# Another phase for the planner's instruction fetches, and shorter 2-KB loads

## The chip, the cores and the metric

One core of a Trainium2 chip runs the whole kernel. The metric is the device time of one execution in microseconds (us), as the median of the runs of a kernel.

## The reference

What is computed is an attention in which a query sees only the keys of its own cluster, and two feed-forward layers behind it. Cut to what matters:

```python
def _attn_ref(q, k, v, centroids):            # q, k, v: 2 x 8 x 768 x 64; centroids: 8 x 16 x 64
    q_assign = np.argmax(np.einsum('bhsd,hcd->bhsc', q_n, c_n), axis=-1)   # q_n, k_n, c_n: rows
    k_assign = np.argmax(np.einsum('bhsd,hcd->bhsc', k_n, c_n), axis=-1)   # of length one
    mask = q_assign[:, :, :, None] == k_assign[:, :, None, :]
    scores = np.where(mask, scale * np.matmul(q, k.transpose(0, 1, 3, 2)), -1e9)
    attn = np.exp(scores - np.max(scores, axis=-1, keepdims=True))
    attn = attn / (np.sum(attn, axis=-1, keepdims=True) + 1e-09)
    return np.matmul(attn, v)
def _moe_ref(x, w_in, w_out):                 # x: 1536 x 512; w_in: 512 x 2048; w_out: 2048 x 512
    h = x @ w_in
    return (h * (1.0 / (1.0 + np.exp(-h)))) @ w_out
def _moe2_ref(x, w_in, w_out, alpha):         # the same shapes
    h = x @ w_in
    return (np.maximum(h, 0.0) + alpha * np.minimum(h, 0.0)) @ w_out
```

The weights come as 64-bit floats, 8 MB for each of the four matrices.

## The kernel before

**Attention.** The work is cut into 96 units, one for a tile of 128 query rows and a head. TensorE makes the scores of a unit from four matmuls (L793 and L797, in `front`): one pair adds the one-hot cluster codes and so the mask, one pair the products. VectorE scales them and takes the minimum (L807), ScalarE takes the exponential (L812) and the high half of the split in two half-precision parts (L819), and VectorE the low half (L821). SyncE then issues a DMA transpose of both parts (L827, in `front_t`), and 18 matmuls with the values (L839, in `back`) read what it wrote. Two units later than the scores, as the code is written, but in the order that a planner sets. Before the units the keys, queries and values are scaled and split and the cluster codes made: K and Q are transposed once for the products (L638, L730) and once with their codes (L684, L746). L498 is a small matmul that sums a scale's squares over the partitions, and its input comes from ScalarE (L611, L648, L713 or L945).

**Weights.** Each of the four weight matrices is loaded in eight pieces of 1 MB (L893). A piece of 64-bit floats is turned into 32-bit ones by ScalarE (L904, L908) and VectorE (L915, L918), scaled by a sum of squares (TensorE's L953 with VectorE's L955 for the first two matrices, ScalarE's L945 for the others), and split in two half-precision parts (L930 on ScalarE, L931 on VectorE).

**Layers.** The first feed-forward layer takes chunks of one or two tiles as soon as their attention is done (matmuls L1187 and L1218, in `layer1`), and the second takes three blocks of 512 rows at the end (L1289 and L1320, in `layer2`). Its results leave by 12 stores (L1328).

**Order.** No engine's order is the one that the code is written in. When all instructions have been recorded, `plan_order` (L313) makes a `Plan`. `data_deps` finds who needs whom, `run` places all instructions by a list schedule with the costs of `costs`, and `improve` repeats this 60 times, forward and backward with a little noise, and keeps the order whose planned end is the earliest. Each engine then runs that order, with SyncE, which issues all DMAs, among them. In `costs` a load has an issue time of 0.47 us, a latency, and a time in the queue by its size and a rate (L104 to L107). In `run` the planner counts TensorE's records, two for each matmul (the weight load and the matmul). When the count passes 256 it takes an instruction fetch to begin. A load or transpose that is then in flight is made later by 1.1 or 0.4 us, and so are those who wait for it and the queue behind it.

Of the kernel before, what the change touches and what calls it, by code (L numbers as in the profile page):

```python
# [48 lines left out]
class Plan:  # L49
# [27 lines left out]
    def costs(self, i):  # L77
        aps = [a for a in list(i.ins) + list(i.outs) if hasattr(a, "bass_ap")]
        n = max(self.size(a) for a in aps) if aps else 1
        kind, e = type(i).__name__, self.engine(i)  # L80
        wide = all(a.dtype in (F16, BF16) for a in aps)
        ptr = sum(hasattr(a, "bass_ap") for a in list(i.ins)[1:]) if n > 1 else 0
        if kind == "InstTensorScalarPtr":
            ptr = sum(self.size(a) == 1 for a in i.ins if hasattr(a, "bass_ap")) if n > 1 else 0
        many = len(list(i.outs)) > 1
        if e == "PE":
            mv = [a for a in i.ins if hasattr(a, "bass_ap")][0]
            return (max(0.025, 0.001 + self.size(mv) * (8 if mv.dtype == F32 else 1) / 2330.0),)
        if e == "DVE":
            if kind == "InstTensorCopy":  # L90
                return (0.15 + n / (3840.0 if wide else 1920.0),)
            if kind == "InstMemset":
                return (0.06 + n / 1000.0,)
            return (0.145 + n / 955.0 + (0.06 * ptr if kind == "InstTensorScalarPtr" else 0) + 0.06 * many,)
        if e == "Activation":
            return (0.19 + n / 1205.0 + 0.09 * min(1, ptr) + (0.06 if many else 0),)
        if e == "Pool":
            if kind == "InstTensorTensor":
                return (0.19 + n / 530.0,)
            return ((0.1 if kind == "InstMemset" else 0.19) + n / 1215.0 + 0.08 * min(1, ptr),)  # L100
        n = max(self.size(a) for a in aps)
        if kind == "InstDmaTransposeAnt":
            return (1.3 if n < 1400 else 1.42, 1.3, n / 750.0)
        rows = [a for a in i.ins][0]  # L104
        run = list(rows.ap)[-1][1] * 4
        rate = 400.0 if run >= 4096 else 290.0 if run >= 2048 else 380.0
        return (0.47, 1.3, n * 512 / 1000.0 / rate)  # L107

    @staticmethod
# [93 lines left out]
    def run(self, prio):  # L203
# [17 lines left out]
        port = [0.0] * ne  # L221
        other = {1: 3, 3: 1}
        window = [0, False, 0.0]
        fetched, flight = 190, []
        for n in range(N):
            if not left[n]:
                heapq.heappush(later[self.eng[n]], (0.0, prio[n], n))
        for _ in range(N):
# [36 lines left out]
            if kind == "PE":  # L265
# [12 lines left out]
                if fetched >= 256:  # L278
                    fetched -= 256
                    flight = [x for x in flight if x[0] > s]  # L280
# [1138 lines left out]
```

## Time and profile before

| | us |
|---|---|
| median of 3 runs (783.64 to 786.57) | 785.26 |
| the profiled execution | 784.7 |
| its span, from the first instruction to the last | 782.8 |
| TensorE (PE) busy | 679.5 |
| VectorE (DVE) busy | 541.3 |
| ScalarE (ACT) busy | 466.5 |
| GpSimd (POOL) busy | 136.2 |

The profile gives busy time by engine, who waited for whom, and for each DMA the time from its issue to its landing. PEld is TensorE's weight load, and SPq the queue of SyncE. An instruction is named by its line in the kernel's file. The granted clock of TensorE is a share of 2.4 GHz: 1.00, or 0.50, which is 1.2 GHz; in between are means over a stretch. The tile "arena" is the one large buffer in which nearly everything lies, so a DMA "arena<-arena" is a transpose. Queue q8 carries the fetches of instructions.

### The profile page before, as it was taken

What the parts mean: (1) busy time and instruction counts of PE and PEld (TensorE: products, weight loads), DVE (VectorE), ACT (ScalarE), POOL (GpSimd) and SP (SyncE); (2) the same over time, 40 slices, a digit from 0 to 9 for tenths busy, and PEclk for the clock granted to TensorE, in tenths of its full rate; (3) what the DMA queues carried; (4) which work ended last, traced back from release to release, by engine and by line L of the source; (5) the groups of instructions that cost most, each with busy time, mean ns of one, the idle gap of its engine ahead of it and who ended that gap; (6) DMA issues with size and microseconds to landing.
All of it is one profiled execution on the core that took longest, in us unless ns stands there. A gap on an engine that the chain in (4) does not pass through costs nothing.

```text
span 782.8 us, 16346 instructions
## 1 busy us (share of the span) xinstructions
PE 679.5 (87%) x6730; PEld 475.0 (61%) x6730; DVE 541.3 (69%) x992; ACT 466.5 (60%) x757; POOL 136.2 (17%) x237
## 2 busy tenths in 40 slices
PE   0254559679999999998999999888999999999998
PEld 0243448568887878887788898774444444444443
DVE  4689998898779578867876886878970385018700
ACT  6875976777778667756765898997640141012200
POOL 3562131123404732121130001000000000000000
PEclk9999978899999999999999999999999999999999
DMA  7989997989999996996898986452000000000000
GB/s 216 300 201 294 300 214 125 156 168 152 165 160 158 186 162 129 155 167 125 138 142 135 243 225 187 160 172 100 1 15 27 14 1 0 28 28 1 0 28 27
DMA packets 241593, 101.85 MB, mean 130 GB/s; under 512 B 217328, under 2 KB 227568, under 8 KB 241392
## 3 DMA queue, kind: packets, MB, share of 16 engines
q1 hardware_dynamic: 241520, 100.83, 60.4%
q8 instruction: 52, 0.85, 0.4%
q14 instruction: 21, 0.17, 0.1%
HBM read 44.08 MB, written 3.15 MB: 60 GB/s over the span
## 4 chain that ended last, share of the span: by engine, by line
PE 36%; ACT 7%; DMA 5%; DVE 2%; issue 1%; POOL 0%; SPq 0%; ACTq 0%
PE w L1320 11%; PE w L1289 10%; PE m L1320 5%; PE m L1289 5%; DMA arena<-in_moe_w_out_dram 2%; PE w L1218 2%; ACT arena L904 2%; ACT arena L908 2%; ACT arena L945 1%; PE w L1187 1%; DMA arena<-arena 1%; DMA arena<-in_moe_w_in_dram 1%; PE x L839 1%; PE s L793 1%; PE s L797 1%
## 5 line engine op out<-in xcount | busy, mean ns | idle before, releaser
L1218 PE MATMUL w<-arena 128*128 128x256 f16 (+1 forms) x1248 | 150.1, 258 | 3.7 <-ACT arena L1225 1.9
L1187 PE MATMUL w<-arena 128*128 128x256 f16 (+1 forms) x1200 | 142.0, 257 | 3.1 <-DVE arena L1195 1.7
L1218 PEld LDWEIGHTS <-arena 128*128 128x128 f16 x1344 | 113.2, 99 | 22.3 <-issue 5.7
L1187 PEld LDWEIGHTS <-arena 128*128 128x128 f16 x1344 | 111.9, 98 | 23.3 <-issue 8.3
L821 DVE TENSOR_TENSOR arena<-arena 128x768 f16<-128x768 f32 x96 | 96.8, 1009 | 30.4 <-ACT arena L819 30.0
L839 PE MATMUL x<-arena 128*128 128x64 f16 x1728 | 108.6, 198 | 10.1 <-DMA arena<-arena 8.0
L812 ACT ACTIVATE arena<-s,stat 128x768 f32<-128x768 f32 x96 | 85.9, 895 | 38.1 <-DVE s L807 18.4
L807 DVE TENSOR_SCALAR_CACHE_REDUCE s<-s,stat 128x768 f32<-128x768 f32 x96 | 97.6, 1019 | 12.2 <-PE s L797 10.4
L839 PEld LDWEIGHTS <-arena 128*128 128x128 f16 x1728 | 90.6, 102 | 21.2 <-DMA arena<-arena 10.9
L819 ACT ACTIVATE arena<-arena 128x768 f16<-128x768 f32 x96 | 80.3, 837 | 30.2 <-DMA arena<-arena 29.5
L1320 PEld LDWEIGHTS <-arena 128*128 128x128 f16 x576 | 56.4, 98 | 68.0
L1289 PEld LDWEIGHTS <-arena 128*128 128x128 f16 x576 | 55.7, 98 | 68.5 <-issue 2.4
L1289 PE MATMUL w<-arena 128*128 128x512 f16 x384 | 94.1, 379 | 0.0
L1320 PE MATMUL w<-arena 128*128 128x512 f16 x384 | 85.8, 379 | 0.0
L1298 DVE TENSOR_SCALAR arena<-w,stat 128x512 f32<-128x512 f32 x32 | 23.9, 747 | 78.8 <-PE w L1289 78.7
L793 PE MATMUL s<-arena 80*128 80x384 f16 x192 | 68.6, 357 | 9.9 <-ACT arena L812 9.7
L1302 ACT ACTIVATE arena<-arena,stat 128x512 f16<-128x512 f32 x48 | 34.4, 718 | 69.2 <-DVE arena L1299 69.2
L797 PE MATMUL s<-arena 128*128 128x384 f16 x192 | 68.5, 357 | 0.0
L450 POOL TENSOR_SCALAR stat<-stat 128x1 int32<-128x1 int32 x49 | 12.4, 256 | 290.1 <-DVE stat L445 197.1
L915 DVE SCALAR_TENSOR_TENSOR arena<-arena 128x1024 int32<-128x1024 int32 x32 | 41.3, 1290 | 22.2 <-ACT arena L908 22.1
L1289 PE MATMUL m<-arena 128*128 128x512 f16 x192 | 51.3, 379 | 0.1
L931 DVE SCALAR_TENSOR_TENSOR arena<-arena,stat 128x1024 f16<-128x1024 f32 x32 | 41.6, 1306 | 5.0 <-ACT arena L930 5.0
(145 smaller groups left out, 969.2 us busy)
## 6 DMA issues: line engine op xcount, KB each, us to landing
arena<-in_moe_w_in_dram SPq DMA_DIRECT2D x16, 1024.0 KB, 6.3
arena<-in_moe_w_out_dram SPq DMA_DIRECT2D x16, 1024.0 KB, 5.9
arena<-in_k_dram SPq DMA_DIRECT2D x8, 384.0 KB, 5.1
arena<-in_q_dram SPq DMA_DIRECT2D x6, 512.0 KB, 5.2
arena<-in_v_dram SPq DMA_DIRECT2D x8, 384.0 KB, 6.2
out_dram<-arena SPq DMA_DIRECT2D x12, 256.0 KB, 2.0
arena<-arena SPq DMA_TRANSPOSE x149, 4.0
arena<-in_moe_alpha_dram SPq DMA_DIRECT2D x1, 1024.0 KB, 5.3
```

Of the source, the lines that this page charges most:

```text
L793: nc.tensor.matmul(out=sc[:, j, :hs], lhsT=qt2[0:D + C, h], rhs=kt2[0:D + C, h % 2, j * hs:(j + 1) * hs], start=True, stop=False,)
L797: nc.tensor.matmul(out=sc[:, j, :hs], lhsT=qt1[:, h], rhs=kt1[:, h % 2, j * hs:(j + 1) * hs], start=False, stop=True,)
L807: nc.vector.tensor_scalar(sc[:, :, :hs], sc[:, :, :hs], nd_cols[:, H * (n % 2) + h:H * (n % 2) + h + 1], None, op0=ALU.mult, op1=ALU.min, ...
L812: nc.scalar.activation(out=view(o, F32, 2, hs), in_=sc[:, :, :hs], func=ACTF.Exp, scale=-1.0, bias=bias, accum_out=sums[n % 2][:, h:h + 1],)
L819: nc.scalar.activation(out=hl[:, 0], in_=p, func=ACTF.Copy)
L821: en.tensor_tensor(out=hl[:, 1], in0=p, in1=hl[:, 0], op=ALU.subtract)
L839: nc.tensor.matmul(out=x_ps[0][:, h], lhsT=pt[:, ph * T + t], rhs=vt[:, h % 2, t, vh], start=(i == 0), stop=(i == 3 * T - 1),)
L931: nc.vector.scalar_tensor_tensor(out=lo, in0=t, scalar=s, in1=hi, op0=ALU.mult, op1=ALU.subtract)
L1187: nc.tensor.matmul(out=hp[:, ff], lhsT=wi[:, a, kd, ff * 128:ff * 128 + 128], rhs=mov(bb, kd), start=(i == 0), stop=(i == 3 * KD - 1),)
L1218: nc.tensor.matmul(out=acc, lhsT=wo[:, a, f % 2, dt * 128:(dt + 1) * 128], rhs=g[:, f, bb], start=(i == 0), stop=(i == 3 * KF - 1),)
L1289: nc.tensor.matmul(out=hp, lhsT=in_piece(o_a + 24 * KB, f // 2)[:, a, kd, f % 2 * 128:][:, :128], rhs=x[bb][:, kd], start=(i == 0), stop=( ...
L1320: nc.tensor.matmul(out=acc, lhsT=g[:, f, a, t * 128:(t + 1) * 128], rhs=out_piece(o_w, f // 2)[:, bb, f % 2], start=(i == 0), stop=(i == 3 ...
```

## The change

Two lines of the planner. The start of its count of records goes from 190 to 50, so that it sees its first fetch at record 206 instead of 66, and all others as much later. The rates by which a load's time in the queue is worked out go from 290 to 350 (GB/s) for rows of 2 KB and from 400 to 395 for rows of 4 KB and more. No instruction is added or taken away, and the planner's order comes out new on every engine.

```diff
@@ costs
-        rate = 400.0 if run >= 4096 else 290.0 if run >= 2048 else 380.0
+        rate = 395.0 if run >= 4096 else 350.0 if run >= 2048 else 380.0
@@ run
-        fetched, flight = 190, []
+        fetched, flight = 50, []
```

Rows of 2 KB are those of the loads of the two input weights (16 loads) and of the 12 stores; the output weights and the broadcast of alpha have longer ones.

Three places of the new order follow. The first is on TensorE, where the matmuls of unit 18 with the values (tile x) begin; w0, w1 are banks of the first layer's results and s0 is a bank of scores. Before, from record 2050:

```order
L1218 MATMUL w0_68<-arena_70 128x128
L1218 LDWEIGHTS arena_70
L1218 MATMUL w1_69<-arena_70 128x128
L839 LDWEIGHTS arena_70
L839 MATMUL x_66<-arena_70 128x64
```

And now, from record 2082:

```order
L793 MATMUL s0_64<-arena_70 128x384
L797 LDWEIGHTS arena_70
L797 MATMUL s0_64<-arena_70 128x384
L839 LDWEIGHTS arena_70
L839 MATMUL x_66<-arena_70 128x64
```

The group has moved from record 2053 to 2085. In the rows where it stood there are now matmuls of L1218.

The second is SyncE's queue near the start, behind the loads of the first keys and queries; L638 and L684 are transposes of the keys, L746 that of the first queries' codes:

```order
-L638 DMA_TRANSPOSE arena<-arena 128x12x128
+L638 DMA_TRANSPOSE arena<-arena 128x12x128 x2
 L893 DMA arena<-in_moe_w_in_dram 128x4x512
-L638 DMA_TRANSPOSE arena<-arena 128x12x128
 L590 DMA arena<-in_v_dram 128x2x384
 L684 DMA_TRANSPOSE arena<-arena 128x12x128
+L893 DMA arena<-in_moe_w_in_dram 128x4x512
 L746 DMA_TRANSPOSE arena<-arena 128x8x128
-L893 DMA arena<-in_moe_w_in_dram 128x4x512 x3
+L893 DMA arena<-in_moe_w_in_dram 128x4x512 x2
```

One of the three weight loads that followed L746 now stands ahead of it, and a transpose of keys stands ahead of the weight load that it followed.

The third is ScalarE up to the first unit's exponential (L812). Before, from the fourth L648 on:

```order
L648 ACTIVATE arena,stat<-arena 128x768
L642 ACTIVATE arena<-arena 128x12x64
L654 ACTIVATE arena<-arena 128x12x64 x2
L1097 ACT_TABLE_LOAD
L1097 ACTIVATE stat<-stat 128x1
L605 ACTIVATE arena<-arena,stat 128x768
L904 ACTIVATE arena<-arena 128x1024
L908 ACTIVATE arena<-arena 128x1024
L812 ACTIVATE arena,stat<-s_65,stat 128x768
```

Now the load of the exponential's table stands behind the third L648:

```order
L611 ACTIVATE arena,stat<-arena 128x768
L648 ACTIVATE arena,stat<-arena 128x768 x3
L1097 ACT_TABLE_LOAD
L1097 ACTIVATE stat<-stat 128x1
L930 ACTIVATE arena<-arena,stat 128x1024
```

And from the fourth L648 on there stand now:

```order
L648 ACTIVATE arena,stat<-arena 128x768
L605 ACTIVATE arena<-arena,stat 128x768
L654 ACTIVATE arena<-arena 128x12x64 x2
L605 ACTIVATE arena<-arena,stat 128x768
L904 ACTIVATE arena<-arena 128x1024
L908 ACTIVATE arena<-arena 128x1024
L654 ACTIVATE arena<-arena 128x12x64
L812 ACTIVATE arena,stat<-s_65,stat 128x768
```

The table load has left the stretch ahead of the exponential, and L642 with it; a scaling (L605) and a copy of values (L654) stand there in their place.

## Rows read from the trace of the kernel before

**Rows 1.** Busy us and instructions by stretch; columns in the first row.

```profile
core 0: us, PE busy (x) PEld busy (x) DVE busy (x) ACT busy (x) POOL busy (x), PEclk, DMA share, GB/s
50.00:130.00 80.00, 50.40 (x598) 38.58 (x598) 75.39 (x157) 58.85 (x83) 24.45 (x36) 0.91 0.98 233
130.00:180.00 50.00, 38.00 (x609) 31.21 (x607) 45.66 (x83) 38.06 (x68) 13.75 (x19) 0.90 0.81 153
180.00:430.00 250.00, 239.97 (x3305) 205.23 (x3302) 191.73 (x388) 174.31 (x318) 66.94 (x99) 0.99 0.91 152
430.00:540.00 110.00, 100.35 (x979) 83.10 (x978) 88.39 (x117) 96.47 (x141) 6.55 (x22) 1.00 0.67 194
540.00:783.00 243.00, 238.95 (x1116) 108.22 (x1113) 109.96 (x165) 60.12 (x92) 1.02 (x6) 1.00 0.04 14
```

**Rows 2.** Waits of PE, 130 to 430: us in total, times, longest.

```profile
PE x L839 <- DMA arena<-arena: 8.0, 8, 2.2
...
PE w L1187 <- DMA arena<-arena: 1.4, 1, 1.4
```

**Rows 3.** Fetches (all; 149.4 to 149.6; 269.0 to 269.1), then busy sums up to two.

```profile
q8 instruction: 52, 0.85, 0.4%
...
q8 instruction: 1, 0.02, 45.8%
...
q8 instruction: 1, 0.02, 55.0%
...
0.00:149.60 149.60, 76.67 (x987) 59.09 (x987) 122.20 (x280) 111.57 (x170) 53.48 (x99) 0.95 0.94 230
0.00:269.10 269.10, 185.72 (x2672) 153.63 (x2673) 218.47 (x465) 204.15 (x338) 93.35 (x155) 0.96 0.96 202
```

**Rows 4.** Two transposes: timeline of SPq, their landing us, PE's timeline behind them.

```profile
143.15 1.42 SPq L827 DMA_TRANSPOSE arena<-arena  x1
...
146.36 1.48 SPq L827 DMA_TRANSPOSE arena<-arena  x1
...
arena<-arena SPq DMA_TRANSPOSE x1, 3.7
...
arena<-arena SPq DMA_TRANSPOSE x1, 5.6
...
152.02 1.14 PE L839 MATMUL x<-arena 128*128 128x64 f16 x18 [2.17 <-DMA arena<-arena]
```

**Rows 5.** Three loads of L893, issued one behind the other, and their landing us.

```profile
L893 SPq DMA_DIRECT2D arena<-in_moe_w_in_dram x3: 446/447/577, 34.1 to 35.3; - x3
...
DMA to landing us min/median/max: 5.9/8.5/11.0
```

**Rows 6.** Start: transpose L746 and its landing, then timelines of PE and ACT.

```profile
L746 SPq DMA_TRANSPOSE arena<-arena x1: 1862/1862/1862, 32.2 to 32.2; - x1
...
DMA to landing us min/median/max: 3.7/3.7/3.7
...
36.99 0.16 PE L498 MATMUL s<-stat,arena 128*128 128x1 bf16 x1 [8.96 <-ACT arena L648]
...
39.16 1.28 ACT L1097 ACT_TABLE_LOAD   x1
...
45.56 0.88 ACT L812 ACTIVATE arena<-s,stat 128x768 f32<-128x768 f32 x1
```

**Rows 7.** Stretches of half the granted clock; columns as in rows 1.

```profile
108.00:122.00 14.00, 9.55 (x92) 6.92 (x92) 14.00 (x25) 9.30 (x15) 2.73 (x3) 0.51 0.67 130
149.20:156.10 6.90, 4.69 (x45) 3.75 (x46) 5.85 (x9) 6.01 (x8) 0.00 (x0) 0.51 1.00 137
166.30:169.70 3.40, 3.40 (x35) 2.73 (x36) 3.16 (x7) 2.00 (x4) 0.00 (x0) 0.50 0.98 189
```

**Rows 8.** Waits of PE, 430 to 540.

```profile
PE s L498 <- ACT arena L945: 4.8, 6, 2.1
```

## The prediction

> **What bounds the kernel now.** I read the sums by stretch first, then TensorE's waits, then the transposes and the instruction fetches, then the start and the end. From 540 us TensorE is busy 238.95 of 243 us and from 180 to 430 it is busy 239.97 of 250 [rows 1]. So the total is TensorE's work plus its idle time, and a new order can only change the idle time and the clock at which the work runs. Idle are 29.6 us in 50 to 130, where VectorE is the bound (75.39 of 80), 12.0 in 130 to 180, 10.0 in 180 to 430 and 9.7 in 430 to 540 [rows 1]. In 130 to 430 the largest named cause is the units' own transposes: TensorE waited 8.0 us ahead of L839 and 1.4 ahead of L1187 for a DMA from the arena to the arena [rows 2]; two smaller kinds I leave out.
>
> Why those transposes come late is to be seen in two of them. One that was issued at 143.2 landed after 3.7 us. The one issued at 146.4 landed after 5.6, and TensorE stood 2.17 us before the matmul at 152.02 that reads it [rows 4]. Between the two ends of the second an instruction fetch of 16 KB ran, in the slice 149.4 to 149.6 [rows 3]. The profile has 52 such fetches [rows 3], one for 256 of TensorE's 13462 records (a weight load and a matmul each), and at the fetch just named TensorE had begun 987 + 987 records, which is 182 beyond a multiple of 256. By 269.1 us, beside another fetch, it had begun 2672 + 2673, which is 225 beyond one [rows 3].
>
> **The change, part by part.** *The count's start.* The planner books a fetch when its count passes 256. With 190 this is at record 66 of each 256, with 50 at record 206. The trace has it at 182 and 225 [rows 3], so the planner of before put every fetch about half a period from its true place, and the changed one puts it right to within some 25 records. What a fetch costs in the planner (0.4 or 1.1 us on a load or transpose in flight) is not changed.
>
> What this moves can be counted in the two orders. I took the first of the 18 matmuls of each unit (L839), which waits for the unit's transpose, and asked how many stand within 80 records behind record 200 of a block of 256, over the 37 blocks from 768 on. It is 28 before and 19 after. Behind record 66, where the old planner saw its fetches, it is 24 before and 35 after. So the move is as meant: units no longer begin just behind a real fetch. The wait at 152.02 is unit 18, whose group stood at record 2053 and now stands at 2085, behind the score matmuls of a later unit.
>
> Price: 8.0 + 1.4 = 9.4 us of waits [rows 2]. If they fall as the count does, by 9 in 28, this is -3.0 us. The bounds are 0 (the wait reappears at the next unit) and -9.4 (the planner now knows the landing and keeps all of them clear). I take -3.0, since the count is the only thing known of the new order at the fetches themselves.
>
> The Trainium skill speaks against this part. Runtime: NRT & Kernel Launch, section Instruction fetch mechanics, says of a refill that "The cost of crossing a 16 KiB boundary is one DMA tail-bump, mostly hidden." By that the term would be 0 and the sum 3.0 us higher. The row on the transpose that took 5.6 us beside 3.7 says otherwise: hidden from TensorE's own instruction stream, perhaps, not from a transpose in flight.
>
> *The clock behind those waits.* Granted clock was half, 1.2 GHz, in 149.2 to 156.1 and in 166.3 to 169.7, with 4.69 and 3.40 us of TensorE work in them [rows 7]. The idle stretch ahead of the first has the fetch waits in it. At 2.4 GHz the same work takes half as long, so at most (4.69 + 3.40) / 2 = 4.0 us are lost there. With the same share of 9 in 28 this is -1.3 us. Bounds: -4.0, and upward one more such stretch; the longest seen, 108 to 122, had 9.55 us of work in it [rows 7], so +4.8.
>
> *The rate of 2-KB rows.* The 16 loads of the two input weights have rows of 2 KB and 1.05 MB each. They were planned at 1.0486 MB / 290 GB/s = 3.6 us and are now planned at 3.0. Of three that queued behind each other the first landed at 34.1 + 5.9 = 40.0 us and the last at 35.3 + 11.0 = 46.3, which is 3.1 a load [rows 5]. So a load was planned 0.5 too long and is now planned 0.1 too short. No engine waits for that by itself; it only moves loads in the order, and that is the next step, so the rate is costed at nothing. The output weights' loads (2.62 to 2.65 us planned) and the stores behind the last matmuls move no other work.
>
> *The start, where both parts act.* In SyncE's queue a weight load now stands ahead of L746, the transpose of the first queries' one-hot, which so far landed 32.2 + 3.7 = 35.9 us [rows 6]. One load more ahead of it is +3.1 us, by the spacing above. TensorE began the first unit only at 36.99 though, since a matmul of L498 ahead of it waited 8.96 us for ScalarE's L648 [rows 6], and this pair stands in the same order after. So 1.1 us of the 3.1 is covered. The other 2.0 meets ScalarE, which reached the first exponential (L812) at 45.56, with the 1.28 us load of its table at 39.16 among what stood between [rows 6]. The table load now stands ahead of that stretch, where ScalarE waited anyhow. If the exponential is held by ScalarE, it comes up to 1.3 us earlier, and if by the transpose, up to 2.0 later. Behind it VectorE is full to 130 us, so either would be passed on. I take 0, since TensorE began the first unit 8.6 us ahead of the exponential; bounds -1.3 and +2.0. If the cover by L648 is gone the price is the whole 3.1.
>
> *The end of the conversions, 430 to 540.* The order of loads there is nearly the same. The waits for L945 were 4.8 us in six, the longest 2.1 [rows 8]. One such wait more or less is the bound: 0, between -2.1 and +2.1.
>
> Sum: -3.0 - 1.3 + 0 + 0 + 0 = -4.3 us. The profiled execution took 784.7 us, of which 782.8 is the span, so 780.4; it lies 0.6 us below the median of 785.3, which gives 781.0. I predict 780.7, between the two.
>
> **The rivals.** *The waits only move (about 785).* What speaks for it: 19 groups of units still stand behind a fetch, and a unit kept clear of one may meet the next. ScalarE also waits for late transposes before it can write the buffer that they read, and that does not depend on where TensorE's group stands. Against it: the count falls where the planner is right and rises where it was wrong. With the count's gain gone and the rest at 0, the time is 784.7 to 785.3. If the skill's rule on fetches held it would be this case too.
>
> *A cold stretch more (about 790).* Place: 100 to 180 us, where TensorE is busy about three quarters of the time and the clock fell three times [rows 1, 7]. The units there have moved by one or two places. Price: a stretch like 108 to 122 costs 4.8 us; where no fetch wait falls away, 785.3 + 4.8 = 790.1. It decides when the new order leaves TensorE idle before such a stretch to the degree that it is in 50 to 130, 50.40 of 80 busy [rows 1]. Against it: the planner models the clock in both versions, and the first matmul of the feed-forward layer stands at record 1194 in place of 1196, so TensorE gets no later a supply.
>
> *A larger gain (about 774).* With the landings right, the planner clears most of the waits: -8 of the 9.4, and with them most of the cold time, -3, so 785.3 - 11 = 774.
>
> **How the numbers follow.** The forecast's case, a saving of some 2.5 to 7 us, has 0.40; the larger gain 0.14; no gain 0.27; a cold stretch more, or a start that comes later, 0.19. A measurement of this kernel can tell about 0.5% from no change, 3.9 us, so faster is below 781.4. All of the larger gain and most of the forecast's case lie there: 0.48. No gain, with the small end of the forecast's case, is 0.33, and slower 0.19. The lower end of the range is 773, at the larger gain with the table load's 1.3 us; the upper end is 790, at the cold stretch. Less than one in ten lies beyond either.
>
> **What would show it.** In the new trace TensorE's waits for the arena's own transposes in 130 to 430 should be about 6.4 us instead of 9.4, with fewer matmuls of L839 found waiting two to three us behind a fetch. The fetches must still come at 170 to 230 records beyond a multiple of 256. The half clock in 140 to 170 should be shorter than 10 us. The first L812 should stand at 44 to 48 us. I am wrong if the waits for DMA fall and the time does not, for then another engine ends the wait last; or if the time falls by more than 5 us with those waits as they were, for then it is the start or the clock alone.

## The result, and the profile after

The changed kernel takes 776.5 us (median of 6 runs, 774.5 to 780.3) beside 784.8 us of the kernel before (783.5 to 787.7). The ratio is 0.989, with a 95% interval of 0.986 to 0.992, so it is faster by 8.3 us. That lies in the range, on the side that was forecast, and 4.2 us below the predicted 780.7.

The profiled execution took 777.4 us, 775.6 of them its span. Its busy times by stretch answer to [rows 1], in the same columns:

```profile
50.00:130.00 80.00, 52.39 (x618) 41.07 (x619) 73.70 (x161) 57.55 (x81) 22.30 (x38) 0.66 0.97 232
130.00:180.00 50.00, 38.60 (x559) 31.13 (x557) 41.95 (x81) 37.23 (x68) 11.90 (x16) 0.83 0.94 161
180.00:430.00 250.00, 240.18 (x3346) 206.81 (x3343) 191.21 (x389) 173.02 (x317) 72.16 (x99) 1.00 0.90 150
430.00:540.00 110.00, 107.17 (x1012) 86.36 (x1011) 92.73 (x125) 100.25 (x150) 9.61 (x22) 1.00 0.68 197
540.00:776.00 236.00, 231.42 (x1079) 104.63 (x1077) 104.83 (x158) 56.59 (x84) 1.01 (x6) 1.00 0.04 14
```

The first column of engines is TensorE. From 180 to 430 us it is idle for 9.8 us, as before (10.0). From 430 to 540 its idle time has gone from 9.7 to 2.8 us: in this one execution 6.8 of the 7.2 us stand in the stretch that the prediction had priced at nothing.

The waits that were to fall are TensorE's for transposes in 130 to 430 [rows 2]. After the change they are:

```profile
PE x L839 <- DMA arena<-arena: 10.6, 12, 2.9
...
PE m L741 <- DMA arena<-arena: 1.4, 1, 1.4
PE m L764 <- DMA arena<-arena: 1.3, 1, 1.3
```

The last two are kinds that the prediction left out. Before they were:

```profile
PE m L764 <- DMA arena<-arena: 0.7, 1, 0.7
...
PE m L741 <- DMA arena<-arena: 0.5, 1, 0.5
```

For L839 it is 10.6 us where 8.0 were before, the wait of L1187 for a transpose is gone, and the two smaller kinds have grown: 13.3 us in all where 10.6 stood. The fetches are where they were in the count. At those of 147.7 and 261.4 us TensorE had begun:

```profile
0.00:147.70 147.70, 76.95 (x986) 60.17 (x987) 120.95 (x283) 112.48 (x171) 50.04 (x101) 0.81 0.97 233
0.00:261.40 261.40, 177.45 (x2524) 146.81 (x2525) 207.93 (x453) 195.78 (x324) 83.73 (x145) 0.86 0.94 199
```

These are 1973 and 5049 records, 181 and 185 beyond a multiple of 256, near the 182 and 225 of [rows 3]. Of the 40 fetches from 120 to 545 us, 27 come at 170 to 230 beyond one, as the prediction expected; the others lie between 151 and 263. So the planner's new count (206) does agree with the chip, though a single fetch may be some 55 records away, and the time fell, but the waits by which the gain was priced did not fall.

Half clock (1.2 GHz, column PEclk) was granted for much longer in this execution than in the profiled one of the kernel before, where it was 24 us in [rows 7] and 3.4 us more, from 289.2 on, that those rows leave out. Now there were five stretches, 72 us in all; the first and the fourth are:

```profile
62.80:107.20 44.40, 26.89 (x275) 19.70 (x274) 41.54 (x88) 34.12 (x44) 10.03 (x17) 0.50 1.13 297
...
144.70:158.40 13.70, 11.29 (x105) 8.49 (x105) 11.37 (x18) 12.12 (x18) 6.79 (x9) 0.50 0.77 118
```

At the start, TensorE waited 2.6 us for the transpose L746 before L764, by its waits in 36 to 50, and by ScalarE's timeline the first exponential began at 44.82, 0.7 us earlier than in [rows 6], released by VectorE:

```profile
PE m L764 <- DMA arena<-arena: 2.6, 1, 2.6
```

```profile
44.82 0.90 ACT L812 ACTIVATE arena<-s,stat 128x768 f32<-128x768 f32 x1 [2.22 <-DVE s L807]
```

In 430 to 540 the wait of [rows 8] has shrunk from 4.8 us to:

```profile
PE s L498 <- ACT arena L945: 1.2, 2, 0.8
```

### The profile page after: what moved, and what is told of

It is laid out like the page before. It is cut to its first block, busy times and chain, and to the rows that moved or that the text cites. A ratio compares the mean times of both kernels' runs of the same rounds, so it can differ in the third digit from the quotient of the medians.

```text
span 775.6 us, 16354 instructions
## 1 busy us (share of the span) xinstructions
PE 680.0 (88%) x6730; PEld 477.4 (62%) x6730; DVE 534.9 (69%) x992; ACT 464.7 (60%) x757; POOL 140.3 (18%) x237
## 4 chain that ended last, share of the span: by engine, by line
PE 53%; DMA 17%; ACT 12%; DVE 8%; issue 6%; POOL 2%; SPq 1%; DVEq 0%; ACTq 0%; POOLq 0%
PE w L1320 11%; DMA arena<-arena 11%; PE w L1289 9%; PE w L1187 7%; PE w L1218 6%; PE m L1320 5%; PE m L1289 4%; PE x L839 3%; PE s L793 3%; PE s L797 3%; DMA arena<-in_moe_w_in_dram 3%; ACT arena L904 2%; ACT arena L908 2%; DMA arena<-in_moe_w_out_dram 2%; DVE s L807 1%
## 5 line engine op out<-in xcount | busy, mean ns | idle before, releaser
L1218 PE MATMUL w<-arena 128*128 128x256 f16 (+1 forms) x1248 | 153.7, 260 | 2.6 <-DVE arena L931 1.7
L1187 PE MATMUL w<-arena 128*128 128x256 f16 (+1 forms) x1200 | 141.9, 257 | 1.4 <-ACT arena L1225 1.4
L1218 PEld LDWEIGHTS <-arena 128*128 128x128 f16 x1344 | 115.9, 100 | 21.6 <-issue 5.0
L1187 PEld LDWEIGHTS <-arena 128*128 128x128 f16 x1344 | 111.6, 98 | 15.8 <-issue 2.1
L839 PE MATMUL x<-arena 128*128 128x64 f16 x1728 | 103.8, 198 | 10.7 <-DMA arena<-arena 10.6
L807 DVE TENSOR_SCALAR_CACHE_REDUCE s<-s,stat 128x768 f32<-128x768 f32 x96 | 97.8, 1021 | 20.1 <-PE s L797 16.3
L812 ACT ACTIVATE arena<-s,stat 128x768 f32<-128x768 f32 x96 | 86.0, 896 | 40.9 <-DVE s L807 23.0
L821 DVE TENSOR_TENSOR arena<-arena 128x768 f16<-128x768 f32 x96 | 94.3, 985 | 20.7 <-ACT arena L819 20.1
L839 PEld LDWEIGHTS <-arena 128*128 128x128 f16 x1728 | 88.0, 101 | 22.2 <-DMA arena<-arena 13.3
L819 ACT ACTIVATE arena<-arena 128x768 f16<-128x768 f32 x96 | 80.6, 839 | 27.9 <-DMA arena<-arena 27.3
L793 PE MATMUL s<-arena 80*128 80x384 f16 x192 | 69.5, 362 | 13.3 <-DMA arena<-arena 8.6
L450 POOL TENSOR_SCALAR stat<-stat 128x1 int32<-128x1 int32 x49 | 18.1, 372 | 265.6 <-DVE stat L445 177.8
L915 DVE SCALAR_TENSOR_TENSOR arena<-arena 128x1024 int32<-128x1024 int32 x32 | 39.4, 1230 | 13.9 <-ACT arena L908 13.5
```

The costliest lines, as they stand in the source:

```text
L793: nc.tensor.matmul(out=sc[:, j, :hs], lhsT=qt2[0:D + C, h], rhs=kt2[0:D + C, h % 2, j * hs:(j + 1) * hs], start=True, stop=False,)
L807: nc.vector.tensor_scalar(sc[:, :, :hs], sc[:, :, :hs], nd_cols[:, H * (n % 2) + h:H * (n % 2) + h + 1], None, op0=ALU.mult, op1=ALU.min, ...
L812: nc.scalar.activation(out=view(o, F32, 2, hs), in_=sc[:, :, :hs], func=ACTF.Exp, scale=-1.0, bias=bias, accum_out=sums[n % 2][:, h:h + 1],)
L819: nc.scalar.activation(out=hl[:, 0], in_=p, func=ACTF.Copy)
L821: en.tensor_tensor(out=hl[:, 1], in0=p, in1=hl[:, 0], op=ALU.subtract)
L839: nc.tensor.matmul(out=x_ps[0][:, h], lhsT=pt[:, ph * T + t], rhs=vt[:, h % 2, t, vh], start=(i == 0), stop=(i == 3 * T - 1),)
```

## The experiments

Four questions were put to the chip: which of the two constants it is, whether the gain lies behind 430 us, whether the fetches' place is the cause or any new order does as well, and how much the planner's own noise moves the time. Each kernel was timed beside the kernel before, which took 785.5 to 785.8 us (medians of the three groups of runs).

### Each constant alone

```diff
-        fetched, flight = 190, []
+        fetched, flight = 50, []
```

> Only the count's start is changed, the rates are those of before. Theory P (the count's start is what tells the planner something new, so the gain is its): about 778 us, that is 785 less most of the 8. Rival R (the loads' rate gives it, since the time that the changed kernel gains lies behind 430 us, where the conversions of the last weights and the loads stand): about 785, no change. Rival D (the result is one draw among new orders, and neither constant has an effect of its own): anywhere from 776 to 787, and the two halves need not add up to -8.

Measured: 769.7 us (768.4 to 771.2), ratio 0.980 [0.978, 0.982]. That is -15.7 us, nearly twice the whole change.

```diff
-        rate = 400.0 if run >= 4096 else 290.0 if run >= 2048 else 380.0
+        rate = 395.0 if run >= 4096 else 350.0 if run >= 2048 else 380.0
```

> Only the rates are changed (350 and 395 GB/s), the count begins at 190 as before. Theory P (the count's start gives the gain): about 784 to 785. Rival R (the rate gives it): about 777 to 778, with TensorE's idle time in 430 to 540 near 3 us in place of 9.7. Rival D (one draw among new orders): anywhere from 776 to 787, and the sum of both halves' differences is not -8.

Measured: 779.7 us (777.3 to 781.9), ratio 0.993 [0.991, 0.995], so -5.7 us. The halves add up to -21 and together they give -8: they don't add, as rival D had it. But the 769.7 us lie 6 below the lowest that D allowed, and 8 below theory P's 778, and the 779.7 us lie between rival R's 777 to 778 and theory P's 784 to 785, with TensorE idle for 8.7 us in 430 to 540 where R wanted 3. No theory had both. The waits of L839 in 130 to 430 say little here. In the run of the count alone (769.7 us), and then in that of the rates alone (779.7), they are:

```profile
PE x L839 <- DMA arena<-arena: 9.4, 9, 1.9
```

```profile
PE x L839 <- DMA arena<-arena: 2.7, 4, 1.3
```

The slower kernel, whose count is wrong, has a third of the waits by which the prediction priced the count.

### The head of one order with the tail of the other

Both orders are planned; each engine takes one of them up to a planned time and then what is left in the order of the other:

```diff
+    for rates, fetched in (HEAD, TAIL):
+        Plan.RATES, Plan.FETCHED = rates, fetched
...
+    order = [[n for n in x if begun[n] < CUT] + [n for n in y if begun[n] >= CUT]
+             for x, y in zip(found[0][1], found[1][1])]
```

> Each engine's order is that of the kernel before up to what its plan begins at 418 us (about 430 us on the chip), and from there the changed kernel's order for all that is left. Theory T (the gain is made by the order behind 430 us: the changed kernel is 1.6 us ahead at the fetch near 424 and 7 ahead at the one near 580): 785 - 6 = 779 us, with TensorE idle for 3 to 4 us in 430 to 540. Rival H (the order of the units ahead of 430 sets it, in that it leaves ScalarE and VectorE with less conversion work at 430, and the tail only shows it): 783 to 786, with TensorE idle for 8 to 10 us there.

Measured: 781.1 us (778.5 to 785.2), ratio 0.995 [0.993, 0.996].

> Each engine's order is that of the changed kernel up to what its plan begins at 414 us (about 425 us on the chip), and from there that of the kernel before for all that is left. Theory T (the gain is made by the order behind 430 us): 785 - 1.6 = 783 us, with TensorE idle for 8 to 10 us in 430 to 540. Rival H (the order of the units ahead of 430 sets it): 777 to 779, with TensorE idle for 3 to 4 us there.

Measured: 782.9 us (781.5 to 788.3), ratio 0.998 [0.996, 1.000]. The stretch 430 to 540 of the first and then of the second:

```profile
430.00:540.00 110.00, 105.09 (x1005) 85.70 (x1003) 89.99 (x123) 96.82 (x142) 8.53 (x22) 1.00 0.66 195
```

```profile
430.00:540.00 110.00, 99.42 (x937) 80.52 (x935) 88.05 (x117) 96.70 (x144) 7.12 (x22) 0.99 0.63 190
```

TensorE is idle for 4.9 us with the new tail and 10.6 with the old one. So the idle time of that stretch does go with its own order, as theory T had it, but the new tail is worth 4.3 us and not 6, and the head 2.6 and not 1.6. The two make 6.9 of the 8.3: the gain is spread over the program. How it is split cannot be read from one execution. The second of these kernels has the changed kernel's order up to about 425 us, and in its profile TensorE had begun 4692 matmuls by 430 us, 49 more than in the changed kernel's own.

### The same order with the fetches elsewhere

This is the sharpest of the tests. The order of the kernel before is kept word for word, and 70 small matmuls are put at TensorE's start, where it is idle for 5 us. A fetch comes with every 256th record, so 140 records more at the start bring each fetch 140 records earlier in the order, to where the old planner saw it. With 128 matmuls (256 records) each fetch is back at its old place; this is the control. The same 70 matmuls ahead of the order with the right count put its fetches wrong.

```diff
+        for _ in range(70):
+            early.append(nc.tensor.matmul(
+                out=bank_w[1][:, :1], lhsT=ones, rhs=ones[:, :1], start=True, stop=True
+            ).ins)
```

> The order of the kernel before, word for word, behind 70 small matmuls (140 records) that TensorE runs first, in its idle time ahead of the first L498 at 5.03 us; they write a bank that nobody reads before it is written anew. All real fetches so come 140 records earlier in the planned order, at about 20 to 110 beyond a multiple of 256, which is where the old planner saw them (66). Theory F (what a plan is worth depends on fetches at their planned place): TensorE's waits for the arena's transposes in 130 to 430 fall from 9.4 to 5 us or less, and the time from 785 to 777 to 782. Rival N (the fetches' place in the order is worth little, and the gain of the changed constants is another order and not a truer one): those waits stay at 7 to 12 us, and the time at 783 to 787.

Measured: 772.7 us (770.9 to 774.4), ratio 0.985 [0.982, 0.988]; 4 us below what theory F expected, and 10 below rival N's.

> The order of the kernel before behind 128 small matmuls (256 records), so that every real fetch comes where it came in the kernel before. This prices the added records by themselves. Both theories: 785 to 787, since 128 matmuls of about 0.03 us end near 5 us and the first L498 begins at 5.03.

Measured: 783.5 us (782.0 to 787.3), ratio 0.999 [0.997, 1.000]; 1.5 us below the expected 785 to 787, so the added matmuls cost nothing that can be seen.

> The order of the run in which only the count's start was changed (769.7 us), behind the same 70 small matmuls. Its real fetches now come half a period from where its planner saw them, as in the kernel before. Theory F: its waits for transposes rise from 12.9 us by several us, and its time from 770 to 773 to 778. Rival N: 769 to 771, and the waits within 10 to 15 us.

Measured: 773.6 us (772.1 to 776.3), ratio 0.987 [0.984, 0.989], where the same order without the matmuls has 0.980 [0.978, 0.982]. This order has no control of its own.

In the order with the right count the named waits hardly tell it: those of TensorE for transposes (L839, L741, L764) go from 12.9 to 14.3 us, which is what rival N expected of them, while the time goes as theory F had it.

So the place of the fetches alone, with no instruction in another order, is worth 783.5 - 772.7 = 10.8 us in the old order and 773.6 - 769.7 = 3.9 us in the other one (5.2 by the two ratios, which come from different groups of runs), each time in the direction of theory F. Rival N falls. Read so, the old order was not a bad one; it was planned for fetches that came elsewhere. But each order was tried with one shift only. That the agreement with the plan is what counts, and not that any shift moves the time by some us, rests on these two directions and on the plans of the other seeds below; other shifts were not tried.

What the profiles of the control and of the moved fetches show of it. (The added lines shift all behind them by 13: L852 is L839, L840 is L827, L832 is L819.) TensorE's waits for the units' transposes in 130 to 430, control first:

```profile
PE x L852 <- DMA arena<-arena: 7.3, 7, 2.1
...
PE w L1200 <- DMA arena<-arena: 1.5, 1, 1.5
```

```profile
PE x L852 <- DMA arena<-arena: 4.9, 6, 1.2
...
PE w L1200 <- DMA arena<-arena: 1.0, 1, 1.0
```

They fall by 8.8 - 5.9 = 2.9 us, not quite to the 5 us that theory F expected, and a quarter of what the time falls by. With TensorE's waits for the other transposes (1.8 us in the control, 0.3 with the fetches moved) the fall is from 10.6 to 6.2, or 4.4 us. Over 115 to 545 us TensorE's idle time falls by 9.9 us, from 32.8 to 22.9 (control first):

```profile
115.00:545.00 430.00, 397.24 (x5095) 332.56 (x5095) 344.05 (x627) 322.78 (x555) 88.84 (x146) 0.98 0.82 160
```

```profile
115.00:545.00 430.00, 407.14 (x5146) 337.90 (x5146) 353.24 (x642) 331.98 (x566) 89.81 (x146) 0.98 0.82 160
```

What the waits for transposes leave of this stands under other names: by TensorE's waits in the same stretch, those for ScalarE go from 14.0 to 11.8 us, for VectorE from 6.3 to 4.2 and for GpSimd from 2.1 to 0.6.

Where it comes from is found when one follows the same instruction in both. VectorE runs the same 992 instructions in the same order (1178 with those that only handle semaphores, by which n counts, from 0); the lag is the start of the n-th in the control less its start with the fetches moved:

| n | 240 | 280 | 340 | 500 | 640 | 780 | 900 | 1000 | 1160 |
|---|---|---|---|---|---|---|---|---|---|
| start in the control, us | 105.5 | 124.9 | 153.2 | 233.0 | 303.4 | 379.2 | 451.3 | 528.8 | 725.9 |
| lag, us | -0.6 | 0.5 | 1.9 | 3.0 | 5.9 | 8.2 | 9.3 | 10.2 | 11.1 |

The lag grows in small steps from about 115 to 545 us and is hardly ever given back. The kernel before, whose fetches are at the control's place, lies behind the control by 1.2 us at n = 240 and 2.0 at n = 640, a level line beside the 6.5 us by which the lag grows over the same stretch.

In the other order (the count's start alone, with the 70 matmuls and without) the lag climbs as well, to 4.3 us near 236 us and to 4.5 near 406, but each time it falls back, to 1.0 us at 333 and to 2.0 at 410, and at the end it is 2.3, which is what the two profiled executions differ by. That order gives most of a delay back, which goes some way to tell why the same shift is worth less there.

One step, around 150 us. In the control a fetch began at 148.2, with two transposes in flight (issued at 145.1 and 146.7) and a third issued 0.2 us later; with the fetches moved there was none between 140.5 and 153.3. Two of these transposes are of L840. Their landing times, control first:

```profile
DMA to landing us min/median/max: 4.9/5.2/5.6
```

```profile
DMA to landing us min/median/max: 3.7/3.8/3.8
```

Behind them, the unit's matmuls on TensorE and the next half on ScalarE, in the control:

```profile
150.75 1.14 PE L852 MATMUL x<-arena 128*128 128x64 f16 x18 [2.14 <-DMA arena<-arena]
...
150.73 0.84 ACT L832 ACTIVATE arena<-arena 128x768 f16<-128x768 f32 x1 [0.86 <-DMA arena<-arena]
```

and with the fetches moved:

```profile
148.27 1.14 PE L852 MATMUL x<-arena 128*128 128x64 f16 x18 [0.40 <-DMA arena<-arena]
...
149.02 0.85 ACT L832 ACTIVATE arena<-arena 128x768 f16<-128x768 f32 x1
```

The numbers in brackets are the idle time ahead of the instruction. Both engines were released by the same landing, 145.1 + 5.6 = 150.7: ScalarE stood 0.86 us because it may not write the buffer that the late transpose still reads, and TensorE 2.14 us for its operand. ScalarE is behind by 1.7 us there (150.73 against 149.02), 1.0 of which is new, and it stays behind.

How many transposes meet a fetch is not what differs. I sorted those issued from 120 to 545 us by whether a fetch began between 0.3 us ahead of their issue and their landing. In the control 61 of 122 did and took 4.9 us in the mean, the other 61 took 3.8. With the fetches moved it was 59 of 122, at 4.7, and 3.9 for the others; with the count alone changed 59 of 121, at 4.8 and 3.9. A late transpose has more time to meet a fetch, so this sorting leans to its side. By a fixed time, the 43 of the control that had a fetch in their first 3.0 us took 4.75 us in the mean, and the 49 that had none in their first 5 us took 3.83: 0.9 us more. With the fetches moved it is 0.6 and with the count alone 0.8. So in each of these three kernels half of the transposes meet a fetch and land that much later. That the order then decides whether something has been left between the late one and its reader is how I read it; one step was followed, not all of them.

The Trainium skill (Runtime: NRT & Kernel Launch, section Instruction fetch mechanics) has the cost of such a fetch as "mostly hidden". By that, moving all of them by 140 records would have left the time as it was. Here it moved it by 10.8 us and by 3.9. Over 52 fetches the 10.8 us are an estimated 0.2 us for each, little for one but not nothing in sum, and the measurement decides.

### Other draws of the planner

```diff
-        noise = Random(1)
+        noise = Random(2)
```

> Only the count's start is changed, and the noise of the 60 rounds of planning begins at another seed (2 in place of 1). Theory P (a count that begins where the fetches are makes a better order, whatever the noise): 767 to 773 us. Rival D (the result is one draw among orders of like worth): anywhere from 768 to 787, most likely 775 to 783.

Measured: 774.3 us (773.9 to 776.9), ratio 0.988 [0.985, 0.990]; 1.3 us above what theory P expected, and still 11 below the kernel before.

> The count's start alone, seed 3. Theory F (a count that agrees with the fetches is worth about 10 us at any seed): 768 to 776. Rival D (769.7 and 774.3 were two lucky draws): 775 to 787.

Measured: 778.4 us (776.4 to 780.4), ratio 0.991 [0.988, 0.995]; outside what theory F expected and within rival D's 775 to 787.

> The changed kernel, both constants, with the planner's noise from seed 2. Its partner with the count's start alone took 774.3 us at this seed. Theory S (with the count right, the rates do nothing of their own, and the 776.5 us of the changed kernel beside 769.7 is the scatter of the planner's draws): within 4 us of 774.3 either way, 770 to 778. Rival R (planning the 2-KB loads 0.6 us shorter makes a worse order wherever the count is right, by about 7 us as at seed 1): 779 to 783.

Measured: 767.5 us (764.2 to 768.0), ratio 0.977 [0.973, 0.980], the fastest of all, 9 us below the changed kernel with its own seed, and below both theories' figures.

> The changed kernel with the planner's noise from seed 3. Theory S (scatter): 769 to 778, and above or below its partner of the same seed. Rival R (the rates cost about 7 us where the count is right): 775 to 783, and 4 us or more above its partner.

Measured: 781.7 us (778.9 to 784.1), ratio 0.994 [0.992, 0.996]; outside theory S's 769 to 778 and within rival R's 775 to 783, but 3.3 above its partner where R wanted 4 or more.

> The kernel before, both constants as they were, with the planner's noise from seed 2. Theory F (a count half a period off costs about 10 us at any seed): 780 to 787, above the 774.3 us of its partner with the count's start moved. Rival D (the seed decides): 770 to 779.

Measured: 783.2 us (the fastest 780.7), ratio 0.997 [0.994, 0.999]; as theory F had it, 8.9 us above its partner.

All plans by their constants (medians, us):

| | seed 1 | seed 2 | seed 3 |
|---|---|---|---|
| count 190, old rates (before) | 785.5 | 783.2 | |
| count 190, new rates | 779.7 | | |
| count 50, old rates | 769.7 | 774.3 | 778.4 |
| count 50, new rates (changed) | 776.5 | 767.5 | 781.7 |

The six plans with the right count have a mean of 774.7 us, the three with the wrong one of 782.8. The count is worth about 8 us, give or take an estimated 3 (from the standard deviations of the six, 5.4 us, and of the three, 2.9). Where seed and rates are the same it is worth 15.7, 8.9 and 3.2 us; across seeds one pair is the wrong way round (781.7 and 779.7). The rates, where the count is right, make +6.8, -6.8 and +3.3 us at the three seeds: nothing of their own that can be seen. The seed by itself moves the time by 9 and by 14 us in the two rows with three seeds, and by 2 in the first. So D is right about the size of the scatter and wrong that there is nothing else.

The waits of L839 in 130 to 430 once more, for seed 2 of the kernel before (783.2 us), of the changed kernel (767.5), and for seed 3 of the count alone (778.4):

```profile
PE x L839 <- DMA arena<-arena: 13.7, 15, 1.9
```

```profile
PE x L839 <- DMA arena<-arena: 8.3, 10, 1.4
```

```profile
PE x L839 <- DMA arena<-arena: 13.7, 12, 1.9
```

13.7 us stand in a kernel of 783 and in one of 778, and 2.7 in one of 780: this sum does not order the kernels.

## Why the prediction was right and wrong

*The count's start (-3.0, bounds 0 and -9.4).* The sign and the cause were right. The planner was half a period off, the change puts it right, and the fetches' place alone is worth 10.8 us in the old order. The step that failed is the price. It took TensorE's named waits for transposes, 9.4 us, as all that there was to gain, and a share of 9 in 28 from where groups stand. With the fetches moved those waits fell by 2.9 us and the time by 10.8. That the 2.9 is close to the -3.0 is luck: in the changed kernel the same waits rose, from 9.4 to 10.6 us. The prediction named what it left out ("ScalarE also waits for late transposes") and used it for a rival only. In the step that was followed, a late transpose holds ScalarE too; ScalarE feeds VectorE, and VectorE the next transpose. The delay then stands in the rows as many short waits under other names, and it adds up. Over 115 to 545 us, ScalarE's own waits for transposes hardly differ in the pair (30.0 us in the control, 28.6 with the fetches moved), but VectorE's for ScalarE's L819 fall from 29.7 to 25.8 us and ScalarE's for VectorE's L807 from 16.7 to 10.5. The bound of -9.4 was too narrow for the same reason.

*What was to show it.* The text expected 6.4 us of such waits after; they are 10.6, and 13.3 with the smaller kinds. Half clock in 140 to 170 was to be shorter than 10 us; it was 13.7. The text also said that a fall by over 5 us with those waits unchanged would mean the start or the clock alone. It was neither: the first exponential came 0.7 us earlier, and the clock gave nothing, as follows. The waits were the wrong witness.

*The clock (-1.3, bounds -4.0 and +4.8).* Not borne out: no gain from the clock can be seen, and no loss. Half clock was granted for 72 us, where the stretches of [rows 7] add up to 24, but such a length is not the order's alone. The control, which has the order of the kernel before and its fetches at the same places, had 58 us of it in its profiled execution. It also cost little: most of it lies in 62.8 to 107.2, where VectorE is busy for 41.54 of 44.40 us and TensorE has time to spare. The 55 executions of the kernel before that were timed beside the experiments say the same. In 31 of them the granted clock was 0.949 to 0.965 over the whole execution, with a median time of 785.7 us, and in the other 24 it was 0.976 to 0.987, with 785.3. The pair with the same order shows it as well. These are their stretches of 50 to 115, control first:

```profile
50.00:115.00 65.00, 36.09 (x417) 26.39 (x415) 63.69 (x129) 48.94 (x63) 21.44 (x30) 0.69 1.01 259
```

```profile
50.00:115.00 65.00, 39.56 (x419) 28.90 (x418) 63.28 (x129) 49.42 (x63) 22.53 (x30) 0.92 1.01 259
```

The mean granted clock is 0.69 and 0.92, VectorE is full in both, and the lag changes by no more than 0.4 us over it. The step that failed is to have priced half clock by TensorE's own work, without asking whether another engine set the pace. What the 13.7 us from 144.7 on cost the changed kernel was not measured.

*The rates (0).* Right in the mean of three seeds. What the term lacked is that any change of a constant is also a new draw, worth up to 7 us either way here.

*The start (0, bounds -1.3 and +2.0).* Right. The transpose came 2.6 us late for TensorE as the text had it (2.0), VectorE's L807 released ScalarE, and the exponential stood at 44.82, within the 44 to 48.

*430 to 540 (0, bounds -2.1 and +2.1).* Wrong: TensorE idles 6.8 us less there. The step read "the order of loads there is nearly the same" as "nothing happens there". Transposes and fetches go on in that stretch. With the same order and the fetches moved, its idle time goes from 8.8 to 5.8 us, so 3 us of such a gain can be the fetches' alone; the rest goes with the new order of the tail, as far as the mixed orders show it (4.9 us idle with the new tail, 10.6 with the old one).

*The sum.* -4.3 was predicted and -8.3 measured. Since the seed alone moves the time by 9 us and more, the exact 776.5 is luck within a gain of about 8, give or take 3, and the range of 773 to 790 would have held four of the six plans with the right count.

*The rivals.* "The waits only move" did happen as a mechanism, at no loss of the gain. The colder stretch came too, at other places, and cost nothing that can be seen.

What stays open: whether shifts other than 140 records follow the plan in the same way, why one order gives a delay back and the other does not, and what in the DMA makes a transpose late by nearly 1 us when a fetch runs beside it. A planner without any fetch in its model was not tried.

## What to carry to other kernels

If an order is planned around a disturbance that comes at regular counts, check the planned place against the trace, and test its worth by shifting the real one with a few idle instructions at the start: no order changes, so with a whole period of the same instructions as the control the difference is the disturbance's alone. Where engines hand work to each other in a loop, don't take the waits of one engine as the most that a delay can cost; follow the same instruction through two runs and see where the lag grows and whether it is ever given back. A change to a planner's constant is judged over several seeds, since one seed here moves the time by as much as the whole change, and the best of a few draws (767.5 us) is a gain by itself.

## What the runs showed of the hardware

A DMA transpose that meets an instruction fetch of TensorE lands nearly 1 us later (in the control 4.9 us in place of 3.8, 61 of each; sorted by a fixed time, 0.6 to 0.9 us in three kernels). That was known from one pair in [rows 4]; that half of all transposes meet one, and that bringing the fetches 140 records earlier moves the time of an order by 4 to 11 us, was not expected. And a lower granted clock, 0.69 in place of 0.92 over 65 us, moved the same order by no more than 0.4 us, in a stretch in which VectorE was busy for 63 to 64 us. Nor did the granted clock of a whole execution, 0.95 to 0.99 for the same kernel, order its times.
